# Turning normalized chunks in squares on VectorE instead of with TensorE, split weight-row transfers, and a new order of the last projections, in a two-layer attention and SwiGLU kernel

## The chip, the cores and the metric

The kernel runs on one core of a Trainium2 chip. A core has five engines that work side by side and meet through semaphores: TensorE (PE, with a separate row PEld for weight loads), VectorE (DVE), ScalarE (ACT), GpSimd (POOL) and SyncE (SP). Each has its own queue and takes its instructions in order. Transfers are issued from an engine's queue (here SP's, some from ACT's) and carried by 16 DMA engines. The metric is the device time of one execution in microseconds, as a median over several runs; less is better.

## The reference

Two layers, each of them attention and then a feed-forward part, both with a residual. There are S = 2048 tokens of D = 448 values, H = 16 heads of 28 values that share one key and one value head, and F = 1792 hidden values.

```python
def layernorm(x):                 # no scale, no shift
    return (x - mean(x)) / sqrt(var(x) + 1e-5)

def attention(x):                 # x: 1 x 2048 x 448
    q = (x @ wq) as 16 heads of 28;  k = x @ wk;  v = x @ wv      # one k, one v
    p = softmax(q @ k.T * 28 ** -0.5)
    return (p @ v, heads joined) @ wo

def feed_forward(x):
    return (silu(x @ w_gate) * (x @ w_up)) @ w_down

for layer in range(2):            # the same weights in both layers
    x = x + attention(layernorm(x))
    x = x + feed_forward(layernorm(x))
```

## The kernel before

All products keep fp32 accuracy by splitting an operand a into a high part (rounded to the type fp32r) and a low part a - high, so that a product is three matmuls: high by high, low by high, high by low. The 448 rows of a transposed activation are held as four tiles k = 0 to 3: three of 128 rows, and one whose lower 64 partitions hold the high part and whose upper 64 the low part of the last 64 rows. The last 64 rows of a weight matrix therefore have to stand on both halves of the partitions; `rows3` (lines 128 to 131) loads the first 384 rows in one transfer (line 130) and the last 64 in a second one whose source is read twice through a leading dimension of stride 0 (line 131):

```python
eng.dma_start(dst[:, 3], src[384:448, :][None].to_broadcast([2, 64, n]))
```

The tokens are cut into NC = 4 chunks of 512. `xres` holds the residual with tokens on partitions. `norm_steps` (line 210) gives the steps of a chunk's layernorm: four of statistics on DVE, one scale on POOL, four that apply it on DVE (line 229), each followed by a POOL copy (line 230) that lays the last 64 columns out twice. `flip` (line 241) turns a normalized chunk for PE: per tile k four PE transposes into one PSUM bank (line 246), a copy that makes the high part (line 252, by ACT, or by DVE if a place is given), and a DVE subtraction for the low part (line 253); the last tile has its own copies and subtraction (lines 256 to 262).

*Start.* x arrives in four transfers of tiles and three of chunks (line 887, SP). `load_wqkv` (line 167) loads wq, wk and wv in two halves, one through ACT's queue and one through SP's, with `rows3`; the casts to the high part are ACT's (line 189), the low parts POOL's or DVE's (line 191). Chunk 0 is normalized and turned, then `project` (line 461) runs 16 projections (c, m): of chunk c the m-th 128 columns, in which 112 belong to four heads of queries and 16 to keys (m = 2, 3) or values (m = 0, 1). The order in a chunk is TURN = (3, 2, 0, 1), keys first. Between the projections stand, by a list of numbers (`at`, lines 317 to 326): loads and splits of keys, stacking of queries (`stack`, `parts`), and `rows` (line 386), which puts a bound of the row maxima into the spare rows of the stacked queries by a transfer (line 391); for the first three stacks all three such transfers come at projection 13. `maxima` (line 393) computes the bounds of a chunk; those of chunk c are made while projection 4c + 6 runs. A value piece is turned by DVE (line 505) and put in place by POOL (line 508).

*Attention* (`scores`, line 528) has 16 units (c, g), a chunk by a group of four heads, each of 16 steps over key tiles. A step is 12 matmuls for the scores (line 565), two ACT exponentials of 512 and 1536 columns (lines 571 and 572) and, two steps later, four matmuls by the values (line 602). After a unit the sums are inverted and spread through three transfers (`post`: rs line 618, rd 628, o 629), and POOL scales and splits the result. After a chunk's fourth unit an output projection (`outproj`, line 544, matmuls at 549) runs between two steps, at kt = 10 of units 4, 8 and 12 (`between_steps`, line 575). Inside it, in units 8 and 12, PE also turns chunk 0 for feed-forward (tiles 0 and 1, then 2 and 3), with copies and subtractions on DVE. The norms of chunks 0, 1 and 2 run beside steps of units 5, 13 and 14.

*Feed-forward* takes the 14 slices of F in seven groups of two. A unit (gi, c, n) is one slice for one chunk: 42 matmuls in pairs side by side on the two halves of the partitions (line 292), ACT's silu (line 825), DVE's product, and later the products by w_down. `scores` ends with the units (0,0,0) and (0,0,1) around the output projection of the last chunk; `rest` (line 856) then turns chunk 1 whole (line 863), and chunks 2 and 3 inside the units (0,1,1) and (0,2,1), in the middle between their two halves of matmuls (`mid`). POOL adds two of four residual tiles per chunk and group (line 743).

The order on every engine is that in which the program text issues the instructions.

## Time and profile before

| | us |
|---|---|
| median of three runs | 2038.59 (2035.05 to 2038.96) |
| the profiled execution | 2040.6 |
| its span, from the first to the last instruction | 2038.9 |
| PE busy | 2015.1 (99%) |
| ACT busy | 1310.6 (64%) |
| POOL busy | 537.7 (26%) |
| DVE busy | 457.7 (22%) |
| mean granted clock of TensorE | 0.996 |

A row of the timeline or of the chain gives the start in us, the duration in us, the engine, the line of the kernel, the operation, the output and inputs by the names of the program, and how many instructions lie in it; in brackets stands the idle time of the engine before it and what ended it. "SPq" and "ACTq" are transfers issued from these queues: their time is that of the issue. A row of a table of groups gives the busy time, the mean of one in ns, and the idle time before. A row of a table of stretches gives the stretch, its length, the busy time of PE, PEld, DVE, ACT and POOL, the granted clock, the busy share of the 16 DMA engines and GB/s. In the chain of waits each piece is what the end of the program waited for at that time. An engine that is busy 99% need not be at its peak, since the ends of matmuls are modelled and matmuls overlap.

### The profile page before, as it was taken

To read this page: it belongs to the slowest core of one execution; us is meant where nothing else is said; L and a number is where in the kernel's file an instruction comes from. 1 tells how busy PE (TensorE), PEld (TensorE's weight loads), DVE (VectorE), ACT (ScalarE), POOL (GpSimd) and SP (SyncE) were. 2 spreads that over 40 slices of the span, in tenths; PEclk is the share of its full clock that TensorE was granted. 3 is DMA by queue.
4 is the path that set the end of the run, shared out by engine and by line. 5 is a ranking of instruction groups with operands and counts; after the bars stand their busy time and mean duration, and the time that the engine had idled before them with its cause. 6 is when DMAs were issued, how large, how long until landed. Compare 5 with 4: busy or idle time off the path is not lost.

```text
span 2038.9 us, 43612 instructions
## 1 busy us (share of the span) xinstructions
PE 2015.1 (99%) x18613; PEld 1271.5 (62%) x18613; DVE 457.7 (22%) x890; ACT 1310.6 (64%) x2152; POOL 537.7 (26%) x601
## 2 busy tenths in 40 slices
PE   8999999999999999999999999999999999999998
PEld 6533434334348999999884334343343689988886
DVE  6200101001114323222461001010011242232322
ACT  3699798997973333333348997979979533333332
POOL 4313121021302333333441221111222123333320
PEclk9999999999999999999999999999999999999999
DMA  5201000011100111100031110000110000111101
GB/s 152 60 22 28 21 13 22 12 37 26 32 12 19 31 31 31 30 17 26 22 93 35 30 30 12 22 12 22 28 45 14 28 16 17 31 31 31 31 1 74
DMA packets 76512, 63.44 MB, mean 31 GB/s; under 512 B 22904, under 2 KB 63224, under 8 KB 76312
## 3 DMA queue, kind: packets, MB, share of 16 engines
q1 hardware_dynamic: 74820, 59.39, 10.4%
q8 instruction: 147, 2.41, 0.5%
q10 hardware_dynamic: 1492, 1.20, 0.2%
q14 instruction: 53, 0.43, 0.1%
HBM read 47.72 MB, written 12.32 MB: 29 GB/s over the span
## 4 chain that ended last, share of the span: by engine, by line
PE 50%; ACT 46%; issue 1%; DMA 1%; DVE 1%; SPq 0%; ACTq 0%; POOL 0%; DVEq 0%; POOLq 0%
PE bank L292 39%; ACT pt L572 31%; ACT pt L571 15%; PE bank L272 5%; PE three L549 2%; PE bank L549 2%; PE bank L246 1%; PE bank L602 0%; PE three L565 0%; DMA wr<-in_A_wk_dram 0%; PE bank L398 0%; DMA qstack<-rows 0%; DMA xres<-in_A_x_dram 0%; DVE xl L253 0%; DVE xn L229 0%
## 5 line engine op out<-in xcount | busy, mean ns | idle before, releaser
L572 ACT ACTIVATE pt<-three 128x1536 f32<-128x1536 f32 x512 | 741.1, 1447 | 0.0
L602 PE MATMUL bank<-pt,vsb 128*32 128x512 f32 x4096 | 546.0, 605 | 0.6 <-ACT pt L572 0.6
L565 PEld LDWEIGHTS three<-qstack,keys 32*128 32x128 f32 x4608 | 252.7, 183 | 450.6 <-ACT pt L571 393.6
L565 PE MATMUL three<-qstack,keys 32*128 32x512 f32 x4608 | 497.8, 425 | 4.1 <-DVE vt L505 2.3
L565 PE MATMUL bank<-qstack,keys 32*128 32x512 f32 x1536 | 492.6, 426 | 0.5 <-ACT pt L571 0.5
L292 PE MATMUL bank<-xh,wgh 64*128 64x512 f32 x1728 | 445.4, 390 | 0.4
L292 PE MATMUL bank<-xh,wgl 64*128 64x512 f32 x1404 | 366.8, 390 | 0.0
L571 ACT ACTIVATE pt<-bank 128x512 f32<-128x512 f32 x512 | 306.0, 598 | 71.6 <-PE bank L565 70.5
L292 PE MATMUL bank<-xl,wgh 64*128 64x512 f32 x1296 | 333.4, 390 | 0.0
L292 PE MATMUL bank<-wdh,h 64*128 64x448 f32 x1792 | 330.8, 364 | 1.5 <-ACT h L827 0.8
L292 PEld LDWEIGHTS bank<-xh,wgh 64*128 64x128 f32 x1728 | 260.9, 184 | 19.5 <-DVE xl L253 1.5
L743 POOL TENSOR_TENSOR xres<-stage,xres 128x448 f32<-128x448 f32 x108 | 127.7, 1204 | 497.8 <-ACT stage L742 497.8
L636 POOL TENSOR_TENSOR o<-o 128x512 f32<-128x512 f32 x32 | 41.1, 1284 | 820.4 <-DMA o<-rd 820.4
L292 PEld LDWEIGHTS bank<-wdh,h 64*128 64x128 f32 x1792 | 241.2, 184 | 15.8 <-issue 2.7
L565 PEld LDWEIGHTS bank<-qstack,keys 32*128 32x128 f32 x1536 | 243.9, 183 | 1.3 <-ACT pt L571 1.1
L299 ACT COPY seen<-bank 128x1 f32<-128x1 f32 x664 | 81.6, 163 | 247.8 <-PE bank L292 245.1
L292 PEld LDWEIGHTS bank<-xh,wgl 64*128 64x128 f32 x1404 | 215.1, 184 | 14.2
L292 PE MATMUL bank<-wdl,h 64*128 64x448 f32 x896 | 216.7, 366 | 0.0
L825 ACT ACTIVATE sg<-bank 128x512 f32<-128x512 f32 x112 | 67.3, 601 | 219.5 <-PE bank L292 214.4
L292 PEld LDWEIGHTS bank<-xl,wgh 64*128 64x128 f32 x1296 | 194.8, 184 | 10.5
L602 PEld LDWEIGHTS bank<-pt,vsb 128*32 128x32 f32 x4096 | 80.8, 108 | 189.9 <-issue 174.2
L826 DVE TENSOR_TENSOR sg<-bank,sg 128x512 f32<-128x512 f32 x112 | 77.5, 692 | 499.4 <-ACT sg L825 490.5
(115 smaller groups left out, 1732.1 us busy)
## 6 DMA issues: line engine op xcount, KB each, us to landing
o<-rd SPq DMA_DIRECT2D x32, 256.0 KB
qd<-stage SPq DMA_DIRECT2D x32, 224.0 KB
qraw<-qd SPq DMA_DIRECT2D x128, 56.0 KB
wdr<-in_B_w_down_dram SPq DMA_DIRECT2D x28, 224.0 KB
wr<-in_B_w_gate_dram SPq DMA_DIRECT2D x28, 192.0 KB
wr<-in_B_w_up_dram SPq DMA_DIRECT2D x28, 192.0 KB
out_dram<-xres SPq DMA_DIRECT2D x15, 224.0 KB
xres<-in_A_x_dram SPq DMA_DIRECT2D x3, 896.0 KB
```

The costliest lines, as they stand in the source:

```text
L272: nc.tensor.matmul(po, a, b, start=(i == 0), stop=(i == len(seq) - 1))
L292: nc.tensor.matmul(po, a, b, start=start, stop=stop, skip_group_check=True)
L299: nc.scalar.copy(seen[:, i : i + 1], po[:, 0:1])
L549: nc.tensor.matmul(po[:, 0:D], a[:, g, ts_], b[:, g, :], start=(g + z == 0), stop=(g == NG - 1 and z == 2))
L565: nc.tensor.matmul(three[:, j, :] if j < 3 else one, k[js, kp, ks], q[js, part, :], start=(z == 0), stop=(z == 2), tile_position=(32 * j, 0),)
L571: nc.scalar.activation(pt1, one, AF.Exp, scale=SCALE)
L572: nc.scalar.activation(pt, three, AF.Exp, scale=SCALE)
L602: nc.tensor.matmul(accs[i][32 * j : 32 * j + 32, :], vsb[:, kt, :], pts[n][j], start=(kt == 0), stop=(kt == NT - 1), skip_group_check=True,)
L636: nc.gpsimd.tensor_tensor(rb, oraw, rb, ALU.mult)
L743: nc.gpsimd.tensor_tensor(r, s, r, ALU.add)
L825: nc.scalar.activation(sg, pg[0], AF.Silu)
L826: nc.vector.tensor_tensor(sg, pg[1], sg, ALU.mult)
```

## The change

Chunks 0, 1 and 2 are turned for feed-forward without PE. Their norms run beside the attention steps of units 5 to 6, 9 to 10 and 13 to 14 (from kt = 6 on, one step of the norm beside each attention step). After the four apply steps come four turning steps, one per tile of 128 tokens: DVE transposes the 128 x 448 tile in squares of 32 x 32, and four transfers on SP's queue write the squares to their places in a DRAM tensor of 448 x 512, in pieces of 32 values. `rows3` loads the turned chunk back. Chunk 0 is loaded and split by POOL beside steps of unit 7; chunk 1 is loaded in unit 15 and split in `rest` by ACT (copies) and DVE (subtractions); chunk 2 is loaded in `rest` and split whole by POOL after the unit (0,1,0). Chunk 3 is turned by PE in unit (0,2,1) as before. The POOL copy of the last 64 columns goes for the three chunks.

`rows3` loads the last 64 rows by two transfers to 64 partitions each, everywhere it is used.

The last chunk's projections come in the order LAST = (1, 0, 2, 3), values first; the three transfers of `rows` are issued at projections 9, 11 and 13.

```diff
--- before.py
+++ after.py
@@ -30,6 +30,7 @@
 LEAD = 4
 LIMIT = 2.0**40
 TURN = (3, 2, 0, 1)
+LAST = (1, 0, 2, 3)
 IDLE = 36
 
 
@@ -126,9 +127,9 @@
         nc.sync.dma_start(dst.bitcast(F32), src.bitcast(F32))
 
     def rows3(dst, src, eng=nc.sync):
-        n = src.shape[1]
         eng.dma_start(dst[:, 0:3], src[0:384, :].rearrange("(k p) n -> p k n", p=P))
-        eng.dma_start(dst[:, 3], src[384:448, :][None].to_broadcast([2, 64, n]))
+        for half in (slice(0, 64), slice(64, 128)):
+            eng.dma_start(dst[half, 3], src[384:448, :])
 
     def split(hi, lo, raw):
         nc.gpsimd.tensor_scalar(hi, raw, 1.0, 0.0, ALU.mult, ALU.add)
@@ -207,7 +208,7 @@
             again,
         )
 
-    def norm_steps(c, pool=pers):
+    def norm_steps(c, pool=pers, twice=True):
 
         got = {}
         cs = slice(4 * c, 4 * c + 4)
@@ -227,7 +228,8 @@
                 got["x"] = pool.tile([P, 4, 512], F32, name="xn")
             o, i, r = got["x"][:, t, 0:D], xres[:, 4 * c + t, :], got["r"][:, t : t + 1]
             nc.vector.tensor_scalar(o, i, mv[:, 4 * c + t, 0:1], r, ALU.subtract, ALU.mult)
-            nc.gpsimd.tensor_copy(got["x"][:, t, D:512], o[:, 384:D])
+            if twice:
+                nc.gpsimd.tensor_copy(got["x"][:, t, D:512], o[:, 384:D])
 
         fs = [lambda t=t: stat(t) for t in range(4)] + [scale]
         return fs + [lambda t=t: apply(t) for t in range(4)], got
@@ -261,6 +263,30 @@
             high = xd[64:128, :]
         nc.vector.tensor_tensor(xh[64:128, k, :], pt[64:128, :], high, ALU.subtract)
 
+    def turn_tile(got, tb, raw, t):
+
+        nc.vector.transpose(tb[:, t, :], got["x"][:, t, 0:D])
+        to = raw.rearrange("(b d) (t g w) -> t g d b w", d=32, g=4, w=32)
+        for g in range(4):
+            nc.sync.dma_start(to[t, g], tb[32 * g : 32 * g + 32, t, :].rearrange("d (b w) -> d b w", w=32))
+
+    def halved(tiles, r, ks, copy, sub):
+
+        xh, xl, xd = tiles
+        for k in ks:
+            if k < 3:
+                copy(xh[:, k, :], r[:, k, :])
+                sub(xl[:, k, :], r[:, k, :], xh[:, k, :], ALU.subtract)
+                continue
+            if xd is None:
+                copy(xh[:, 3, :], r[:, 3, :])
+                high = xh[64:128, 3, :]
+            else:
+                copy(xd[64:128, :], r[64:128, 3, :])
+                copy(xh[0:64, 3, :], r[0:64, 3, :])
+                high = xd[64:128, :]
+            sub(xh[64:128, 3, :], r[64:128, 3, :], high, ALU.subtract)
+
     def product_T(po, a_h, a_l, tiles):
 
         xh, xl = tiles[:2]
@@ -307,7 +333,7 @@
             self.layer = layer
             self.X, self.norms, self.qd = {}, {}, {}
             self.done = 0
-            self.order = [(c, m) for c in range(NC) for m in TURN]
+            self.order = [(c, m) for c in range(NC) for m in (TURN if c < NC - 1 else LAST)]
             self.seen = 0
             self.steps, self.places = [], []
             self.lent, self.plan = None, {}
@@ -320,7 +346,7 @@
                 self.at(4 + 3 * i, lambda i=i: self.stack(i))
                 self.at(6 + 3 * i, lambda i=i: self.parts(i))
                 if not full:
-                    self.at(13, lambda i=i: self.rows(i))
+                    self.at((9, 11, 13)[i], lambda i=i: self.rows(i))
             if not full:
                 self.at(2, self.first_keys)
                 self.at(3, self.diagonal)
@@ -464,7 +490,7 @@
             for f in self.plan.get((self.seen, 0), ()):
                 f()
             late = self.layer == 0 and self.seen == 3
-            turned = [o[0] for o in self.order[self.seen : self.seen + 2] if o[1] == 3]
+            turned = [self.order[n][0] for n in (self.seen, self.seen + 1) if n % 4 == 0 and n < len(self.order)]
             for o in turned if not late else ():
                 self.turned(o)
             self.q(c, m)
@@ -584,12 +610,9 @@
                     if not todo or kt != 10:
                         return
                     c = todo.pop()
-                    ks = list({8: (0, 1), 12: (2, 3)}.get(i, ()))
                     adds = []
                     for t in (1, 2, 3):
                         adds.append(outproj(c, t, free[:, t - 1, :]))
-                        if ks:
-                            flip(got, X0, [ks.pop(0)], one)
                     for f in adds:
                         f()
                     outproj(c, 0, one)()
@@ -641,10 +664,40 @@
                     return rest
 
                 X0 = xtile(xpool)
-                fs, got = norm_steps(0)
-                fs1, got1 = norm_steps(1)
-                ff.norms[1] = got1
-                ff.second = norm_steps(2)
+
+                def turns(c, got):
+
+                    at_ = {}
+
+                    def one(t):
+                        if t == 0:
+                            at_["tb"] = wp.tile([P, 4, D], F32, name="tb")
+                        turn_tile(got, at_["tb"], ff.raw[c], t)
+
+                    return [lambda t=t: one(t) for t in range(4)]
+
+                def back():
+
+                    at_ = {}
+
+                    def load():
+                        at_["r"] = pers.tile([P, 4, 512], F32, name="xn")
+                        rows3(at_["r"], ff.raw[0])
+
+                    def part(k):
+                        halved(X0, at_["r"], [k], nc.gpsimd.tensor_copy, nc.gpsimd.tensor_tensor)
+
+                    return [load] + [lambda k=k: part(k) for k in range(4)]
+                aside = {}
+                for c in range(NC - 1):
+                    fs, got = norm_steps(c, twice=False)
+                    ff.raw[c] = dram.tile([D, 512], F32, name=f"xt{self.layer}_{c}")
+                    fs += turns(c, got)
+                    for n, f in enumerate(fs):
+                        aside[16 * (4 * c + 5) + 6 + n] = f
+                for n, f in enumerate(back()):
+                    aside[16 * 7 + 2 + 3 * n] = f
+                aside[16 * 15 + 2] = lambda: ff.fetch(1)
                 last = NT * len(GR)
                 for n in range(last):
                     i, kt = divmod(n, NT)
@@ -671,9 +724,8 @@
                         between_steps(n)
                     if n in due:
                         due.pop(n)()
-                    if i in (5, 13, 14) and kt > 5:
-                        for f in {5: fs, 13: fs1, 14: ff.second[0][:5]}[i][kt - 6 : kt - 5]:
-                            f()
+                    if n in aside:
+                        aside[n]()
                 for n in (last - 2, last - 1):
                     pv(n)
                 self.lent = None
@@ -698,6 +750,7 @@
             self.layer, self.X, self.W, self.norms = layer, {}, {}, {}
             self.pend, self.soon, self.dn, self.flip, self.mid, self.left = [], [], {}, 0, {}, []
             self.nxt = Attention(1) if layer == 0 else None
+            self.raw, self.got = {}, {}
 
         def down(self, fs, fc, d, hh, hl):
 
@@ -776,6 +829,16 @@
             if c < 2:
                 self.mid[len(groups) - 1, c + 2, 0] = [lambda ks=ks: flip(got, a.X[c], ks) for ks in ((0, 1), (2, 3))]
                 self.soon.append([2, lambda: [a.project() for _ in range(2 - c)]])
+
+        def fetch(self, c):
+
+            self.got[c] = pers.tile([P, 4, 512], F32, name="xn")
+            rows3(self.got[c], self.raw[c])
+
+        def parts(self, c, copy, sub):
+
+            self.X[c] = xtile(self.xbp, self.xd[c])
+            halved(self.X[c], self.got.pop(c), range(4), copy, sub)
 
         def turned(self, c, ks=range(4)):
             if c not in self.X:
@@ -860,14 +923,14 @@
             self.xd = [xd.tile([P, 512], F32R, name=f"xd{c}") for c in range(NC)]
             dma(self.xd[0][64:128, :], self.X[0][0][0:64, 3, :])
             self.X[0] = (*self.X[0][:2], self.xd[0])
-            self.turned(1)
-            fs2, self.norms[2] = self.second
+            self.parts(1, nc.scalar.copy, nc.vector.tensor_tensor)
             fs3, self.norms[3] = norm_steps(3)
-            for f in fs2[5:] + fs3[:5]:
+            for f in fs3[:5]:
                 f()
+            self.fetch(2)
+            self.soon.append([0, lambda: self.parts(2, nc.gpsimd.tensor_copy, nc.gpsimd.tensor_tensor)])
             self.soon.append([1, lambda: [f() for f in fs3[5:]]])
-            for c in (2, 3):
-                self.mid[0, c - 1, 1] = [lambda c=c, ks=ks: self.turned(c, ks) for ks in ((0, 1), (2, 3))]
+            self.mid[0, 2, 1] = [lambda ks=ks: self.turned(3, ks) for ks in ((0, 1), (2, 3))]
             for gi, fs in enumerate(groups):
                 if self.layer == 1 and fine is not None and gi in (2, 3):
                     self.verdict(gi == 3)
```

## The prediction

> **What bounds the kernel now.** I read the page's shares first, then the chain of waits, then stretches of the trace around the three kinds of place that the change touches: the start, the two starts of attention, the two passages into feed-forward.
>
> ```profile
> span 2038.9 us, 43612 instructions
> ...
> DMA packets 76512, 63.44 MB, mean 31 GB/s; under 512 B 22904, under 2 KB 63224, under 8 KB 76312
> ...
> q1 hardware_dynamic: 74820, 59.39, 10.4%
> ...
> PE 50%; ACT 46%; issue 1%; DMA 1%; DVE 1%; SPq 0%; ACTq 0%; POOL 0%; DVEq 0%; POOLq 0%
> ```
>
> Half of the chain is PE (projections, feed-forward), the other half is ACT's exponentials in attention; DMA, DVE and POOL hardly appear. So work moved to DVE, POOL or DMA is paid only where it makes PE or ACT wait, and time can be won only where PE or ACT waits now. These stretches show where (PE, weight load, DVE, ACT and POOL busy, then clock, DMA share and GB/s):
>
> ```profile
> 8.00:10.00 2.00, 0.36 (x2) 0.17 (x2) 1.02 (x3) 0.00 (x0) 1.39 (x3) 1.00 0.14 46
> 16.00:22.00 6.00, 5.79 (x13) 4.29 (x14) 5.68 (x11) 3.05 (x7) 2.90 (x9) 0.50 0.56 179
> 74.00:78.00 4.00, 4.00 (x21) 2.00 (x16) 1.28 (x2) 2.44 (x3) 0.58 (x1) 0.50 0.13 34
> 625.00:627.00 2.00, 2.00 (x22) 1.71 (x20) 1.90 (x7) 0.42 (x4) 0.00 (x0) 1.00 0.15 46
> ```
>
> In the first, only the transfers of last weight rows (line 131) are on their way, and 0.14 of the DMA engines' time is used, about 2 of 16; at 625 us, with the same form under way, 0.15. In the second and third PE runs at half clock.
>
> **A. The start.** The chain and the rows of the start:
>
> ```profile
> 5.76 9.54 DMA wr<-in_A_wk_dram
> ...
> 16.21 13.27 PE bank L272 x44
> ```
> ```profile
> 8.02 5.72 SPq L887 DMA_DIRECT2D xres<-in_A_x_dram  x3
> ...
> 13.43 0.94 ACT L189 CAST wh<-wr 128x896 fp32r<-128x896 f32 x1 [5.61 <-DMA wr<-in_A_wq_dram]
> ...
> 14.45 2.50 POOL L191 TENSOR_TENSOR wl<-wr,wh 128x896 fp32r<-128x896 f32 x2 [3.39 <-ACT wh L189]
> 15.38 0.30 ACT L189 CAST wh<-wr 128x128 fp32r<-128x128 f32 x1 [1.01 <-DMA wr<-in_A_wk_dram]
> 15.58 1.55 ACT L252 CAST xh<-bank 128x512 fp32r<-128x512 f32 x3
> ```
> ```profile
> 9.55 2.91 PE L246 MATMUL bank<-ident,xn 128*128 128x128 f32 x16 [2.08 <-DVE xn L229]
> 16.21 0.79 PE L272 MATMUL bank<-xh,wh 128*128 128x512 f32 x1 [3.75 <-ACT xh L252]
> ...
> 29.08 0.39 PE L272 MATMUL bank<-xh,wl 128*128 128x512 f32 x1
> ```
>
> PE has turned chunk 0 by 12.46 and then idles 3.75 us: ACT's copies of xh stand in its queue behind the casts of the weights, and these wait for the two row transfers, landing near 13.3 and 15.3. The change puts two transfers of 64 partitions in the place of each such broadcast. If both spread over all engines, they land soon after the large parts. The large part of wq landed by about 8.0 (the first of the three xres loads, behind it, was issued at 8.02), and the extra issues on ACT's queue, about 0.55 us each, move its table load from 6.33 to about 9. Then the casts run from about 10.5 (0.94 and 0.30), the xh copies start near 11.8 instead of 15.58, wl is there near 14.0 (10.5 + 0.94 + 2.50) and the third matmul, which reads wl, starts near 14.05; it starts at 17.53 now (16.21 + two at half clock). That is 3.5 us. The half clock comes after the idle stretch; with PE's wait cut to short pieces it need not come, and then the 44 matmuls of chunk 0 go at some 0.23 us (those of the end of the row) and end near 23.6 instead of 29.4: 5.8 us. Bounds: 0 (the rows land as late, or the x loads, issued earlier, take the engines) and -6.2; I take -5, nearer the second, since 0.14 busy with both row transfers open leaves them nothing to share. The Trainium skill, "DMA: Bandwidth & Descriptors", Rules for kernel authors, says that a leading broadcast of c copies keeps a DMA to c engines; the shares 0.14 and 0.15 agree with c = 2. In the same table it advises against two transfers to halves of the partitions, since they serialize; by that sentence alone the step would be worth nothing.
>
> Every later weight load has seven issues where it had five, but SP is mostly idle there and the loads lie tens of us ahead: 0.
>
> **B and C. The two starts of attention.** Layer 0, then layer 1:
>
> ```profile
> 66.16 1.94 SPq L391 DMA_DIRECT2D qstack<-rows  x3
> ...
> 70.02 0.59 ACT L498 COPY stage<-bank 128x512 f32<-128x512 f32 x1
> ...
> 71.56 0.50 PE L565 MATMUL three<-qstack,keys 32*128 32x512 f32 x3 [2.06 <-DVE vt L505]
> ```
> ```profile
> 72.57 0.60 ACT L571 ACTIVATE pt<-bank 128x512 f32<-128x512 f32 x1 [1.96 <-PE bank L565]
> ...
> 81.24 0.60 ACT L571 ACTIVATE pt<-bank 128x512 f32<-128x512 f32 x1 [1.01 <-PE bank L565]
> ...
> 83.13 0.60 ACT L571 ACTIVATE pt<-bank 128x512 f32<-128x512 f32 x1
> ```
> ```profile
> 1074.35 2.48 SPq L391 DMA_DIRECT2D qstack<-rows  x3
> ...
> 1080.04 0.51 PE L565 MATMUL three<-qstack,keys 32*128 32x512 f32 x3 [1.76 <-DMA qstack<-rows]
> ...
> 1081.06 0.60 ACT L571 ACTIVATE pt<-bank 128x512 f32<-128x512 f32 x1 [0.76 <-PE bank L565]
> ```
>
> In both, step 0 waits for the first of three row transfers, all issued after projection 13, some 5.5 us before (1074.35 to 1080.04), and for the last V piece on DVE. The change issues them after projections 9, 11 and 13 and puts V ahead of the keys among the last four projections. Then step 0 follows the last projection, and ACT's first exponential follows its last copy: in layer 0 near 70.6 (70.02 + 0.59) for 72.57, 2.0 us. The half clock between 73 and 80 delays steps 1 to 4: the fifth exponential starts at 83.13, while at the later pace of 1.9 us (81.24 to 83.13) it would start at 70.6 + 4 x 1.9 = 78.2. Without the half clock B is thus worth 4.9. Bounds -2.0 and -5.0; I take -4.5, since layer 1 with a gap of 1.76 keeps its clock and here no gap is left. Layer 1: the last copy of ACT has still to wait for its buffer, so the exponential comes at about 1079.4 to 1079.9 instead of 1081.06: bounds -1.0 and -2.0, taken -1.5. The keys of chunk 3 come last now; they are needed at step 12, 12 x 1.9 = 23 us on, and take about 13 (store and load at some 5.6 each, by the row transfer of layer 1, and a POOL split of 1.9, rows under E): 0. The Trainium skill, "TensorE: Matmul & The Clock Gate", Part 1, says that a whole idle window of 3.4 us halves the clock and a busy one restores it. The trace agrees that it is lost after 3.75 us of idling and back some 6.7 us later; a gap of 2.06 costs it in layer 0 and 1.76 does not in layer 1.
>
> **D. Flips of chunk 0 inside the output projections.** The steps without and with flips:
>
> ```profile
> 228.50 0.60 ACT L571 ACTIVATE pt<-bank 128x512 f32<-128x512 f32 x1 [10.35 <-PE bank L565]
> ...
> 361.23 0.60 ACT L571 ACTIVATE pt<-bank 128x512 f32<-128x512 f32 x1 [11.04 <-PE bank L565]
> ```
>
> Here ACT waits for PE, 0.69 us longer with two flips. Four such places go: -2.8 (bounds -2.4 and -3.2).
>
> **E. The passages into feed-forward.** Chunks 1 and 2 come back from DRAM; chunk 3 is still turned by PE.
>
> ```profile
> 618.88 1.91 PE L246 MATMUL bank<-ident,xn 128*128 128x128 f32 x16
> 620.88 1.09 PE L292 MATMUL bank<-xh,wgh 64*128 64x512 f32 x2
> ```
> ```profile
> 627.84 0.60 ACT L825 ACTIVATE sg<-bank 128x512 f32<-128x512 f32 x1 [1.96 <-PE bank L292]
> ...
> 637.58 0.60 ACT L825 ACTIVATE sg<-bank 128x512 f32<-128x512 f32 x1 [1.29 <-PE bank L292]
> ...
> 645.32 0.60 ACT L825 ACTIVATE sg<-bank 128x512 f32<-128x512 f32 x1 [1.96 <-PE bank L292]
> ```
> ```profile
> 630.33 2.33 POOL L743 TENSOR_TENSOR xres<-stage,xres 128x448 f32<-128x448 f32 x2 [1.31 <-ACT stage L742]
> ```
> ```profile
> L134 POOL TENSOR_SCALAR qstack<-qraw 128x512 fp32r<-128x512 f32 x32 | 20.0, 624 | 0.2
> L135 POOL TENSOR_TENSOR qstack<-qraw,qstack 128x512 fp32r<-128x512 f32 x32 | 41.2, 1288 | 2.7
> ```
>
> The 16 transposes before unit (0,1,0) go, but ACT's first copy must wait for the last output projection, whose weights lie in the memory that chunk 1 takes; PE then waits about 1 us instead of turning for 2: -1.0. The 16 transposes inside unit (0,1,1) go too: from silu to silu (line 825) it takes 9.74 us, the next unit without flips 7.74, so -2.0. Against this, POOL splits chunk 2 whole, behind its two adds for chunk 0 (end about 631.6 in the shifted time): three times 0.62 + 1.29, two more copies and a subtraction, 8.3, with gaps some 8.6, so until 640.2. Unit (0,2,0) would begin near 635.6 (1.0 after the silu at 637.58, shifted by 3.0) and needs the third tile's low part seven pairs of matmuls on, at 0.23 each, so at 637.2, where it waits 0.4 (637.6); two pairs later, at 638.1, it needs the last tile and waits 2.1: +2.5. Sum per layer -0.5, bounds -2 (POOL faster than its rows in attention) and +3.5 (the gap of 2.1 halves the clock for some 6.7 us, about 3.4 more, and some tenths of gaps on POOL). Twice: -1, from -4 to +7.
>
> **F. What is added to attention.** Per layer DVE gets 12 transposes (0.72 us by the row of 128x512) and 12 fewer passes at other places; POOL four splits of 1.9 us; SP 48 writes of 448 pieces of 128 bytes. DVE is busy 457.7 us and POOL 537.7 of 2038.9, and a step has 1.9 us set by ACT, so the work itself is hidden. For the writes: 0.104 of 16 engines' 2038.9 us over 74820 packets is 45 ns each; a chunk's 7168 pieces over 16 engines are then 20 us of queue, in a burst of 8 us. Behind it stand qstack loads, which are issued a unit (30 us) ahead, and the chain of sums of an output (rs, rd, o), which has as long before its output projection. Price 0; if each small write took four times as long, the cover would be gone (below).
>
> **Sum.** -5 - 4.5 - 1.5 - 2.8 - 1 + 0 = -14.8 us on the profiled execution of 2040.6 us, which lies 2.0 above the median of 2038.59; I take the sum off the median: 2023.8, told as 2024. A change of 0.2%, 4 us, is about what a measurement of this kernel can tell from none.
>
> **Rivals.**
> 1. *The start gains nothing*, because ACT waits elsewhere or the x loads now compete with the weights: 2024 + 5 = 2029. For it: the row transfer of wk is small and could be late because its queue was, not its engines. The Trainium skill's advice against halves, told above, would end here too.
> 2. *POOL's split of chunk 2 becomes the bound of the passage* and takes the clock with it: +3.5 per layer in the place of -0.5, 2032. For it: POOL is one engine with 8.6 us of work against some 6.5 of cover (631.6 to 638.1).
> 3. *Slower: the small writes hold the queues.* If a 128-byte write costs four times 45 ns, a chunk's burst takes 80 us, and with 30 us for the unit that it falls in and 30 for the next, which the lead of the queries covers, 20 are left in which ACT waits: for six bursts 120, so 2144. It decides from some three times the 45 ns, where a burst outgrows 60 us; 2.3 us beyond that in each eat the whole gain. Against it: 22904 of the packets are under 512 bytes already and the mean is still 45 ns. The Trainium skill, "DMA: Bandwidth & Descriptors", Specifications, has writes under 512 bytes as read-modify-write, which speaks for it; no row here tells their price apart.
> 4. *PE's flips were no bound*: the places of D are filled by other waits: 2024 + 2.8, 2027. Against it: the two rows under D differ by just the flips.
>
> **How the numbers follow.** Chances: the sum as taken, with its terms inside their bounds, 0.50; rival 1, 0.13; rival 2, 0.13; rival 4, 0.07 (all faster); 1 and 2 together, about 2037, no change, 0.06; rival 3 or a milder form of it, 0.11. That gives faster 0.83, same 0.06, slower 0.11. The likeliest case alone spans 2017 to 2030 (A, B and E at their ends, not all at once). Up to 2036 it takes in rivals 1, 2 and 4: range 2016.5 to 2036.
>
> **What would show it.** A: PE's first projection near 12.5 and its 44 near 23.6, no half clock from 16 to 22. B, C: no row transfer before step 0, exponentials near 60 to 65 in shifted time and 1.9 us apart from the first on. D: ACT's idle of 10.35 at all three places of a layer. E: unit (0,1,1) in 7.5 us, then PE waiting for POOL in (0,2,0). F: steps in the units where turns run stay at 1.9 us, and the transfers of rd and qraw land as before; steps longer than that in those units would make the prediction wrong by rival 3.

## The result, and the profile after

The changed kernel takes 2024.96 us (median of five runs, 2024.49 to 2026.19) against 2038.59 for the kernel before. The ratio is 0.9935, with a 95% interval of 0.992 to 0.9949. The forecast was 2024, faster. The profiled execution took 2026.0 us and its span is 2024.3.

These lines of the page of the changed kernel answer to those of before: the span, the packets of all queues, the largest queue (q1, 71.20 of 75.24 MB), and the shares of the chain.

```profile
span 2024.3 us, 43691 instructions
...
DMA packets 126336, 75.24 MB, mean 37 GB/s; under 512 B 69656, under 2 KB 109976, under 8 KB 126136
...
q1 hardware_dynamic: 124584, 71.20, 13.1%
...
PE 48%; ACT 47%; issue 1%; DMA 1%; POOL 1%; DVE 1%; ACTq 0%; POOLq 0%; SPq 0%; DVEq 0%
```

There are 46752 more packets under 512 bytes, and the chain still consists of PE and ACT; POOL has come in with 1%. Where the time went is read by setting marks of the two traces side by side. Each row is the start of the same piece of work; the column before the last is what the stretch up to it gained or lost, and the last one what was forecast for it.

| mark | before | after | shift | this stretch | forecast |
|---|---|---|---|---|---|
| second run of PE flips at the start | 29.31 | 23.88 | -5.43 | A: -5.4 | -5 |
| fifth exponential, layer 0 | 83.13 | 72.63 | -10.50 | B: -5.1 | -4.5 |
| unit (0,0,0) of feed-forward, layer 0 | 595.88 | 583.61 | -12.27 | D and F: -1.8 | -1.4 |
| feed-forward after the passage, layer 0 | 652.51 | 642.43 | -10.08 | E: +2.2 | -0.5 |
| first exponential, layer 1 | 1081.06 | 1069.54 | -11.52 | C: -1.4 | -1.5 |
| unit (0,0,0) of feed-forward, layer 1 | 1601.31 | 1587.85 | -13.46 | D and F: -1.9 | -1.4 |
| feed-forward after the passage, layer 1 | 1657.94 | 1644.02 | -13.92 | E: -0.5 | -0.5 |
| end of the span | 2038.9 | 2024.3 | -14.6 | the rest of feed-forward and the last transfers: -0.7 | 0 |

The start, from PE's timeline and from ACT's:

```profile
12.31 0.50 PE L298 MATMUL bank<-xh,wh 128*128 128x512 f32 x1
13.04 0.51 PE L298 MATMUL bank<-xl,wh 128*128 128x512 f32 x1 [0.23 <-DVE xl L255]
14.23 0.50 PE L298 MATMUL bank<-xh,wl 128*128 128x512 f32 x1 [0.69 <-POOL wl L192]
```
```profile
9.25 1.28 ACT L964 ACT_TABLE_LOAD   x1 [9.25 <-DMA wr<-in_A_wk_dram]
10.54 0.20 ACT L964 ACTIVATE warm<-halfn 128x1 f32<-128x1 f32 x1
10.65 1.12 ACT L190 CAST wh<-wr 128x896 fp32r<-128x896 f32 x2
11.68 1.55 ACT L254 CAST xh<-bank 128x512 fp32r<-128x512 f32 x3
```

The casts start at 10.65 instead of 13.43, and PE's gap of 3.75 us has become two of 0.23 and 0.69. The stretches show the clock; the columns are as in the table of before:

```profile
16.00:22.00 6.00, 6.00 (x28) 4.99 (x27) 4.44 (x14) 2.57 (x5) 2.54 (x6) 1.00 0.65 218
...
74.00:78.00 4.00, 4.00 (x48) 1.32 (x40) 0.00 (x0) 4.00 (x5) 1.52 (x2) 1.00 0.01 2
```

PE runs at full clock in both, where it had 0.50 before. The starts of attention (ACT, layer 0 and layer 1):

```profile
65.07 0.61 ACT L597 ACTIVATE pt<-bank 128x512 f32<-128x512 f32 x1
...
72.63 0.60 ACT L597 ACTIVATE pt<-bank 128x512 f32<-128x512 f32 x1
...
1069.05 0.59 ACT L524 COPY stage<-bank 128x512 f32<-128x512 f32 x1 [0.22 <-DMA qd<-stage]
1069.54 0.60 ACT L597 ACTIVATE pt<-bank 128x512 f32<-128x512 f32 x1
```

No exponential of these waits for PE any more; the first one follows ACT's own last copy. At the output projections ACT waits as long in unit 8, where chunk 0 was turned, as in unit 4, and even a little less (unit 12 as unit 8: 10.08, for 11.02 before):

```profile
217.90 0.60 ACT L597 ACTIVATE pt<-bank 128x512 f32<-128x512 f32 x1 [10.34 <-PE bank L591]
...
349.81 0.60 ACT L597 ACTIVATE pt<-bank 128x512 f32<-128x512 f32 x1 [10.08 <-PE bank L591]
```

The passage into feed-forward lost time in layer 0. PE in unit (0,2,0) waits three times for POOL's split of chunk 2:

```profile
625.71 0.50 PE L318 MATMUL bank<-xl,wgh 64*128 64x512 f32 x2 [1.07 <-POOL xl L279]
627.06 0.71 PE L318 MATMUL bank<-xh,wgh 64*128 64x512 f32 x1 [0.61 <-POOL xh L286]
628.39 0.79 PE L318 MATMUL bank<-xh,wgh 64*128 64x512 f32 x1 [0.63 <-POOL xh L288]
```
```profile
628.00:632.00 4.00, 3.61 (x18) 3.41 (x20) 1.78 (x4) 0.53 (x4) 1.85 (x5) 0.50 0.01 4
1628.00:1632.00 4.00, 1.99 (x13) 0.82 (x9) 0.66 (x1) 0.00 (x0) 3.79 (x4) 1.00 0.00 0
```

The second row of the stretches is layer 1. The same three gaps stand there (1.07, 0.61 and 0.85), and the clock stays at 1.00 in and after them; in layer 0 it falls to 0.50, and unit (0,2,0) takes 13.4 us from silu to silu (621.83 to 635.25) instead of 10.9 (1625.96 to 1636.83).

### The profile page after: what moved, and what is told of

The parts are those of the page before. It is cut to its first block, busy times and chain, and to the rows that moved or that the text cites. A ratio compares the mean times of both kernels' runs of the same rounds, so it can differ in the third digit from the quotient of the medians.

```text
span 2024.3 us, 43691 instructions
## 1 busy us (share of the span) xinstructions
PE 2001.9 (99%) x18517; PEld 1263.2 (62%) x18517; DVE 453.8 (22%) x890; ACT 1305.1 (64%) x2142; POOL 561.4 (28%) x611
## 2 busy tenths in 40 slices
DMA packets 126336, 75.24 MB, mean 37 GB/s; under 512 B 69656, under 2 KB 109976, under 8 KB 126136
## 3 DMA queue, kind: packets, MB, share of 16 engines
q1 hardware_dynamic: 124584, 71.20, 13.1%
## 4 chain that ended last, share of the span: by engine, by line
PE 48%; ACT 47%; issue 1%; DMA 1%; POOL 1%; DVE 1%; ACTq 0%; POOLq 0%; SPq 0%; DVEq 0%
PE bank L318 38%; ACT pt L598 32%; ACT pt L597 15%; PE bank L298 5%; PE three L575 2%; PE bank L575 2%; PE bank L248 1%; POOL xl L279 0%; PE bank L625 0%; DMA qd<-stage 0%; PE three L591 0%; PE bank L424 0%; DMA xn<-xt 0%; DMA xres<-in_A_x_dram 0%; DMA wr<-in_A_wk_dram 0%
```

## The experiments

The theory is the forecast's sum of separate places. Its rivals are that the halves of a transfer gain nothing, that one of the two edits at the start of attention does all, that the PE turns taken out of feed-forward were worth more than POOL's split, and that the small writes hold the queues. All times are medians; the kernel before took 2039.4 to 2040.6 in these groups of runs. The changed kernel was timed in another group, in which the kernel before took 2038.59. So "more than the changed kernel" sets two groups side by side, and a difference of 1 to 2 us told in this way decides nothing without the traces.

### The row transfers alone

```diff
-        eng.dma_start(dst[:, 3], src[384:448, :][None].to_broadcast([2, 64, n]))
+        for half in (slice(0, 64), slice(64, 128)):
+            eng.dma_start(dst[half, 3], src[384:448, :])
```

> The kernel before with only the row transfers split in two halves of 64 partitions. My reading: the broadcast keeps the transfer to 2 of 16 DMA engines, and the two halves use all of them, so the casts of the first weights start near 10.6 us instead of 13.4, PE's 44 projections of chunk 0 end near 24.0 instead of 29.4, no half clock from 16 to 22, and nothing else moves: 5.4 us less, 2033. Rival (halves serialize and gain nothing): the casts start where they did, 2038.6. Second rival (the gain of the start comes from something else in the change): also 2038.6, with the rows landing earlier.

Measured: 2033.86 us against 2039.59, ratio 0.9972 (0.9962 to 0.9982), so 5.7 less. In the stretches of this run the start is that of the changed kernel:

```profile
8.00:10.00 2.00, 0.64 (x5) 0.21 (x3) 1.02 (x3) 0.78 (x1) 1.39 (x3) 1.00 0.26 30
16.00:22.00 6.00, 6.00 (x28) 4.99 (x27) 4.44 (x13) 2.58 (x5) 2.53 (x6) 1.00 0.66 223
1076.00:1080.00 4.00, 4.00 (x16) 2.12 (x16) 0.00 (x0) 3.61 (x4) 2.56 (x5) 0.50 0.12 38
```

The two halves carry the whole of term A. They do so in eight of the nine traced executions of kernels that have them, where the first cast starts at 10.5 to 10.9; the ninth is told below, with the three buffers. The third line is a surprise: this profiled execution (2038.62) lost the clock at the start of attention in layer 1, with a gap of 1.91 us, where the kernel before with 1.76 kept it; the other eight executions took 2032.4 to 2034.8.

The Trainium skill, "DMA: Bandwidth & Descriptors", Rules for kernel authors, advises against two transfers to halves of the partitions. Here the measurement decides otherwise: the choice was between two halves and one broadcast of two copies, which the skill's same table keeps on two engines, and the halves won 5.7 us.

### Early row transfers, values first, and both

```diff
-                    self.at(13, lambda i=i: self.rows(i))
+                    self.at((9, 11, 13)[i], lambda i=i: self.rows(i))
```

> The kernel before with only the three row transfers of the stacked queries issued at projections 9, 11 and 13; the last chunk still projects keys first. My reading: two waits end together at step 0, the row transfer and the last value piece on DVE (71.43 in layer 0), so taking one away leaves the other: step 0 in layer 0 at 71.4 to 71.6 as before, half clock as before; in layer 1 step 0 earlier, but step 1 still behind the value piece at 1081.1, so at most 0.7 us. Sum 0 to -1, 2038. Rival (the row transfer alone was the wait): 2038.6 - 6.5 = 2032.

Measured: 2034.84 us, ratio 0.9977 (0.9967 to 0.9986), 4.8 less. My reading was wrong for layer 0: this edit alone has most of the gain. PE's timeline of this run, layer 0:

```profile
70.00 0.50 PE L565 MATMUL three<-qstack,keys 32*128 32x512 f32 x3
...
72.06 0.50 PE L565 MATMUL three<-qstack,keys 32*128 32x512 f32 x3 [1.09 <-DVE vt L505]
```

Step 0 follows the last projection at once: it never waited for the value piece, though the row of before named DVE. The piece's bank belongs to step 1, which waits 1.09 us for it. A gap of 1.09 instead of 2.06 kept the clock, and the fifth exponential starts at 78.96 instead of 83.13. For layer 1 the reading was right that step 1 stays behind the value piece, and the wait there is longer (PE's timeline, then a stretch):

```profile
1074.19 0.50 PE L565 MATMUL three<-qstack,keys 32*128 32x512 f32 x3
...
1077.20 0.50 PE L565 MATMUL three<-qstack,keys 32*128 32x512 f32 x3 [2.04 <-DVE vt L505]
```
```profile
1078.00:1080.00 2.00, 2.00 (x12) 1.16 (x4) 0.00 (x0) 1.48 (x3) 1.83 (x3) 0.50 0.00 1
```

This execution, the slowest of ten (2037.6, the others from 2033.5), lost the clock after 2.04 us behind the value piece. So the new order has a task of its own: it takes away the wait of step 1, of 1.09 us in layer 0 and 2.04 in layer 1.

```diff
+LAST = (1, 0, 2, 3)
-            self.order = [(c, m) for c in range(NC) for m in TURN]
+            self.order = [(c, m) for c in range(NC) for m in (TURN if c < NC - 1 else LAST)]
```

> The kernel before with only the order of the last chunk's projections changed (values first); the row transfers are all issued at projection 13. My reading: step 0 still waits for the row transfer, 5.5 us after projection 13, so exponentials start where they did (72.6, 1081.1), half clock in layer 0 as before: 0 to -0.5, 2038.4. Rival (the value piece on DVE was the wait, as the row of step 0 in layer 0 says): -5 in layer 0, -1.4 in layer 1, 2032.

Measured: 2037.0 us, ratio 0.9983 (0.9974 to 0.9993), 2.6 less. The ten executions lie from 2033.85 to 2039.44, four of them above 2037.5. The profiled one (2039.14) shows the wait for the row transfer, shorter by 0.7 (the transfers are issued at 65.08 for 66.16), and the half clock after it:

```profile
70.60 0.50 PE L566 MATMUL three<-qstack,keys 32*128 32x512 f32 x3 [1.32 <-DMA qstack<-rows]
```

In layer 1 of the same execution the wait is 1.20 us and the clock is kept. So the gap that remains seems small enough to cost the clock in some executions only. That is an inference from the spread: the others have no trace.

Both diffs together:

> The kernel before with both: early row transfers and values first. My reading: the two waits go together, step 0 follows the last projection, no half clock after it in layer 0 (5.1 us), and 1.4 us in layer 1: 6.5 us less, 2032. If the half clock comes without a gap too, 2.0 + 1.4 = 3.4 less, 2035. If either of the two edits alone gives this, its own run shows it.

Measured: 2033.51 us, ratio 0.9972 (0.9961 to 0.9982), 6.1 less, with exponentials 1.9 us apart from the first one on in both layers. The two edits do not add up to the sum of what each does alone (4.8 and 2.6): each by itself shortens the gap of layer 0 to one that kept the clock (1.09) or seems to keep it in some executions (1.32), and that is won once.

### The changed kernel without its row transfers

```diff
-        for half in (slice(0, 64), slice(64, 128)):
-            eng.dma_start(dst[half, 3], src[384:448, :])
+        eng.dma_start(dst[:, 3], src[384:448, :][None].to_broadcast([2, 64, n]))
```

> The changed kernel with the row transfers as broadcasts again. My reading: the start goes back to the idle of 3.7 us and the half clock, 5.4 us more, 2030.4, and nothing else moves except that the clock may be kept or lost at other places (2.5 either way). Rival (the parts hide one another): less than 3 more.

Measured: 2031.88 us, ratio 0.9958 (0.9942 to 0.9973), 6.9 more than the changed kernel. The half clock of the start is back, and in the profiled execution it also comes in the passage of both layers, with the same three gaps. A is separate from the rest; the surplus of 1.5 is not explained. In the two traces the start makes 5.8 of it all (the first exponential after the output projection of unit 4 comes at 223.72 for 217.90), and the passages, by where the clock is lost, take 1.0 in layer 0 and add 1.5 in layer 1; only one execution of each kernel has a trace.

### Chunk 2: by PE again, and split by two engines

```diff
-            self.fetch(2)
-            self.soon.append([0, lambda: self.parts(2, nc.gpsimd.tensor_copy, nc.gpsimd.tensor_tensor)])
-            self.mid[0, 2, 1] = [lambda ks=ks: self.turned(3, ks) for ks in ((0, 1), (2, 3))]
+            for c in (2, 3):
+                self.mid[0, c - 1, 1] = [lambda c=c, ks=ks: self.turned(c, ks) for ks in ((0, 1), (2, 3))]
...
+            for f in fs2[5:] + fs3[:5]:
```

> The changed kernel with chunk 2 turned by PE inside unit (0,1,1), as in the kernel before; chunks 0 and 1 stay as changed. My reading: 16 transposes come back (2.0 to 2.4 us a layer), the waits for POOL go (2.3 a layer, and 2.5 of half clock in layer 0): together 3 less, about 2022; this piece of the change would then cost time. Rival (the transposes taken away were worth more than POOL's waits): 4 more, 2029.

Measured: 2022.36 us, ratio 0.9915 (0.9901 to 0.9928), 2.6 less than the changed kernel. Taking chunk 2 off PE was a loss, as it was done. The traces agree: from the silu of unit (0,1,0) to that of (0,2,0) it takes 17.48 us here in layer 0 and 17.49 in layer 1, and 20.71 and 18.17 in the changed kernel, so 0.7 more where the clock stays and 3.2 where it falls. If the parts add up, this also prices the turning of chunks 0 and 1: 17.0 less than the kernel before, less 5.7 and 6.1, leaves 5.2 for the four places in the output projections and the two of chunk 1.

```diff
-            self.soon.append([0, lambda: self.parts(2, nc.gpsimd.tensor_copy, nc.gpsimd.tensor_tensor)])
+            self.soon.append([0, lambda: self.parts(2, nc.gpsimd.tensor_copy, nc.vector.tensor_tensor)])
```

> The changed kernel with chunk 2 split by two engines: POOL makes the copies, DVE the subtractions. My reading: in both layers PE waits at unit (0,2,0) for POOL's split (1.07 + 0.61 + 0.63 us), and in layer 0 these three gaps also cost the clock for some 6 us (2.5 us). With five copies of 0.62 on POOL from 619.3 and subtractions of 0.69 on DVE the last tile is there near 622.8, before PE asks for it at 624.6: no wait, no half clock: 2.3 + 2.5 and 2.3, about 7 less than the changed kernel, 2018. If the clock is lost there only in some executions, 5 to 7 less. Rival (the wait is for something other than POOL's subtractions, the loads say, or DVE is as late): no gain, 2025.

Measured: 2017.8 us, ratio 0.989 (0.9875 to 0.9906), 7.2 less than the changed kernel. This beats both kernels. In PE's timeline of this run, from 616 to 640, no row has a wait; DVE's shows the four subtractions:

```profile
619.99 3.10 DVE L279 TENSOR_TENSOR xl<-xn,xh 128x512 fp32r<-128x512 f32 x3 [2.21 <-POOL xh L278]
623.12 0.98 DVE L288 TENSOR_TENSOR xh<-xn,xd 64x512 fp32r<-64x512 f32 x1
624.14 0.69 DVE L889 TENSOR_TENSOR sg<-bank,sg 128x512 f32<-128x512 f32 x1
```

The last tile is there at 624.1 instead of 628.34, and PE reads it at 624.88. In POOL's subtractions lay the 2.3 us of waits in layer 0 and the 2.5 in layer 1, and in layer 0 the 2.5 us of half clock: layer 1 has no wait at this place either, and the clock stays at both.

```diff
+            if c == 1:
+                self.X[2] = xtile(self.xbp, self.xd[2])
-            self.X[c] = xtile(self.xbp, self.xd[c])
+            if c not in self.X:
+                self.X[c] = xtile(self.xbp, self.xd[c])
```

> The kernel with chunk 2 split by POOL and DVE, and with chunk 1's tiles for feed-forward in the second of three buffers instead of the first. My reading: the first copy of chunk 1 waits for the last output projection only because its tile lies where the weights of that projection lie (0.71 + 0.23 us of PE idle a layer); if the second buffer is free earlier, the copies run beside the projection and PE goes on at once: 1.9 less, 2016. Rival (the second buffer lies under something that is needed as long): 2017.8, no change.

Measured: 2017.28 us, ratio 0.989 (0.9875 to 0.9905): no change against the kernel it is built on. PE still waits 0.71 us ahead of unit (0,1,0), for a copy that still waits for the last output projection. The rival fits, but what lies under the second buffer stays open.

The profiled execution (2019.69, the others 2017.1 to 2017.5) shows something else, at the start. ACT's cast of wk, then PE's first projection:

```profile
14.03 0.30 ACT L190 CAST wh<-wr 128x128 fp32r<-128x128 f32 x1 [1.83 <-DMA wr<-in_A_wk_dram]
```
```profile
14.86 0.80 PE L298 MATMUL bank<-xh,wh 128*128 128x512 f32 x1 [2.08 <-ACT xh L254]
```

The two halves of wk were issued at 8.72 here, 0.6 us later than in the changed kernel's trace (8.10), while the loads of x followed at 9.29 for 9.15; from 12 to 14 the DMA engines are busy throughout in both. PE's first projection is 2.6 us later than there (12.31), and the clock, which fell to 0.50 during the transposes, is at 0.50 from 12 to 18. This looks like the forecast's first rival, x loads that compete with the weights, in one of nine traced executions; that the x loads are the reason is not shown.

### What the small writes cost

```diff
-        for g in range(4):
+        for g in (0, 1, 2, 3) * 4:
             nc.sync.dma_start(to[t, g], tb[32 * g : 32 * g + 32, t, :].rearrange("d (b w) -> d b w", w=32))
```

> The changed kernel with every square written four times over to the same place (192 transfers of 448 pieces of 128 bytes a layer for 48, more work than needed). My reading: a write costs some 17 ns of a DMA engine by the difference of the two profiles, so four times a chunk's writes are 30 us of queue and 38 us of issues on SP, and the lead of one to two units (30 us each) still covers them: 0 to 2 more, up to 2027. The rival of small writes that hold the queue: some 20 us more for each burst that outgrows 60 us, 2050 to 2150.

Measured: 2048.94 us, ratio 1.0043 (1.0028 to 1.0059), 24 more than the changed kernel and more than the 2 expected. SP's timeline of this run during the turning of chunk 0, then that of the changed kernel:

```profile
252.89 20.19 SPq L271 DMA_DIRECT2D xt<-tb  x32
273.12 2.48 SPq L641 DMA_DIRECT2D rs<-o  x4
275.70 19.93 SPq L271 DMA_DIRECT2D xt<-tb  x32
295.67 0.48 SPq L651 DMA_DIRECT2D rd<-rs  x1
```
```profile
252.93 4.05 SPq L271 DMA_DIRECT2D xt<-tb  x8
261.44 2.47 SPq L641 DMA_DIRECT2D rs<-o  x4
264.03 4.46 SPq L271 DMA_DIRECT2D xt<-tb  x8
268.60 0.44 SPq L651 DMA_DIRECT2D rd<-rs  x1
```

The row sums of unit 4 (rs, then rd) stand in SP's queue between and behind the squares. With four writes rd is issued 27 us late, and the units after it make up a part of that. In the output projection of unit 8 PE waits 6.39 us for POOL's split of the result, the clock falls to 0.50, and ACT's idle is 9.6 us longer than the 10.08 of the changed kernel:

```profile
359.10 0.60 ACT L597 ACTIVATE pt<-bank 128x512 f32<-128x512 f32 x1 [19.70 <-PE bank L591]
```

The same places of unit 12 and of layer 1 add 1.9, 7.7 and 2.4 us, and the passage of layer 1, which loses its clock here, 2.5. The next runs ask whether SP's issues or the DMA engines are to blame.

```diff
+            for _ in range(3):
+                nc.sync.dma_start(to[t, g][:, 0, :], tb[32 * g : 32 * g + 32, t, 0:32])
```

> The changed kernel with as many transfers as when every square is written four times (192 a layer), but the added 144 write only one block of 32 x 32 each, 32 pieces for 448. It tells SP's issues from the writes themselves. My reading after the run with four full writes (24 more): there SP issued for 43 us on end and the row sums of the unit came out behind it, while the pieces cost some 14 ns of an engine each, 25 us a chunk; so it is SP's queue, and this kernel loses as much, 2045 to 2049. Rival (the small writes hold the DMA engines): most of the 24 us go, 2025 to 2030.

Measured: 2311.29 us, ratio 1.133 (1.1309 to 1.135). This run does not compare as meant: each added transfer writes into a place just written and waits until that has landed, 1.3 us in the mean (362.5 us over 288 waits), with all of SP's queue behind it. SP then issues from 253.1 to 339.8, 87 us. It does show that few pieces (138408 packets in all against 258216 with four full writes) and a queue occupied for longer cost far more than many pieces in a queue occupied for less.

```diff
+    spare = dram.tile([6 * 48, 32, 32], F32, name="spare")
...
+            for z in range(3):
+                nc.sync.dma_start(spare[made[0] + 12 * t + 3 * g + z], tb[32 * g : 32 * g + 32, t, 0:32])
```

> As the kernel with 144 added small writes a layer, but these go to places of their own in a spare tensor, so that none waits for another to land. SP issues 64 transfers a chunk, as with four full writes, and the DMA engines get 16 x 448 + 48 x 32 = 8704 pieces for 28672. If SP's queue is what held the row sums (my reading), SP is busy some 25 to 43 us on end and the loss is like that of four full writes or somewhat less, 10 to 24, so 2035 to 2049. If the small writes hold the DMA engines, nearly all of the loss goes, 2025 to 2028.

Measured: 2032.97 us, ratio 0.9965 (0.9952 to 0.9978), 8.0 more than the changed kernel: below the 10 to 24 that I expected, and above the rival's. In the trace it is 5.7 more, of which the output projections make 3.6 (2.5 in layer 0, 1.0 in layer 1), and the clock in the two passages 1.5. The stretch from 281 to 285, in the middle of the burst, the issue of rd and the wait at unit 8 follow:

```profile
281.00:285.00 4.00, 4.00 (x48) 1.31 (x40) 0.00 (x0) 4.00 (x5) 0.00 (x0) 1.00 0.24 38
```
```profile
290.49 0.37 SPq L658 DMA_DIRECT2D rd<-rs  x1
```
```profile
352.54 0.60 ACT L604 ACTIVATE pt<-bank 128x512 f32<-128x512 f32 x1 [12.61 <-PE bank L598]
```

The DMA engines are busy a quarter of the time in this stretch, and rd is still issued 22 us late, and ACT's idle at the output projection is 2.5 us longer. The transfers behind rd are not slower either. POOL's product of unit 4 waits for them, in the changed kernel and with four full writes:

```profile
275.68 1.29 POOL L659 TENSOR_TENSOR o<-o 128x512 f32<-128x512 f32 x1 [25.15 <-DMA o<-rd]
```
```profile
302.69 1.28 POOL L659 TENSOR_TENSOR o<-o 128x512 f32<-128x512 f32 x1 [52.20 <-DMA o<-rd]
```

From the issue of rd to this product it is 7.1 and 7.0 us, and 6.9 with the spare tensor (290.49 to 297.39). So the burst delays the chain only by holding back the issue of rd in SP's queue, and the loss follows that time: 268.6 (changed kernel), 290.5 (8 more), 295.7 (24 more), 339.8 (286 more).

```diff
-        for g in range(4):
+        for g in (0, 1, 2, 3) * 2:
```

> The changed kernel with every square written twice: 32 transfers a chunk, some 22 us of SP for 12, and 14336 pieces. It asks how much cover the turning has. With four writes the row sums came 27 us late and the output projection waited 9.5 us, so some 17 us are covered; with two the row sums are late by some 10: 0 to 1 more than the changed kernel, 2025 to 2026. If the cover is less than one such burst: 4 to 8 more, 2030.

Measured: 2026.2 us, ratio 0.9935 (0.9918 to 0.9951), 1.2 more than the changed kernel, in another group of runs; the two profiled spans are 2024.4 and 2024.3. rd is issued at 275.4, 7 us late, and no wait at an output projection grows (10.10 for 10.08 in unit 8). The cover is between 7 and 22 us of SP's queue beyond what the changed kernel uses.

## Why the prediction was right, and where not

**The sum.** -14.8 was forecast for the profiled execution and -14.6 came. That it came so near is luck: B and D gave 1.5 more than said and A 0.4, E gave 2.7 less in layer 0, and the end added 0.7 that nothing in the change explains. The mechanisms of A, C and D and of E's waits are those of the forecast; one sentence under B and the price of D failed, and the half clock of E came in one layer only.

**A** (-5; -5.4 in the trace, -5.7 alone) came step by step: casts near 10.5 (10.65), xh copies near 11.8 (11.68), the third matmul near 14.05 (14.23), no half clock. The rival that the start gains nothing is out for the median by its own run; one traced execution in nine had a late transfer of wk, as this rival has it.

**B** (-4.5; -5.1) was right in size, but the forecast's sentence that step 0 also waits for the last value piece on DVE failed. With early row transfers alone step 0 follows at once in both layers; the value piece held step 1, by 1.09 us in layer 0 and 2.04 in layer 1. The row of step 0 named the engine whose event came last, and the other layer's row named the transfer; the run with one edit decided it.

**C** (-1.5; -1.4) came as worked out: ACT's last copy waits for its buffer (0.22), then the exponential.

**D** (-2.8; -3.7 with F) was mis-sized: the two rows set unit 8 with flips beside unit 4 without, but unit 8 without flips is quicker than unit 4 (10.08 for 10.34), so a place was worth 0.94 to 1.08, 4.0 in all, and not 0.69. Rival 4 is out with it.

**E** is where rival 2 came true in one of two layers. POOL's split ended at 628.34; the forecast's 640.2, less the 12.3 that the trace is ahead there, is 627.9. The waits sum to 2.3 and 2.5 for a forecast of 2.5, and where the clock stays the layer comes out at -0.5, as said (layer 1). That the gap halves the clock was kept as a bound and a rival, at 3.4 us; it measured 2.5 from silu to silu, in layer 0 alone. The run with PE turning chunk 2 and the run with DVE subtracting show both halves of the account. The forecast's own terms for chunk 2, -2.0 and +2.5, already made this piece a loss.

**F** (0): set against the 4.0 of D, the stretches with turns lose some 0.1 to 0.2 us a layer. Rival 3 was right to look at SP and the small writes, but its mechanism failed: a write costs 17 ns of an engine by the two profiles ((0.131 x 2024.3 - 0.104 x 2038.9) x 16 over the 49764 packets that q1 has more), less than half the mean of 45 that the forecast took, and 14 by the run with four writes. What decides is the 0.5 to 0.6 us that SP takes for each issue, and the cover is not the 60 us that the rival allowed but some 7 to 22 beyond the present use.

## What to carry to other kernels

A transfer that reads its source twice through a leading dimension of two used 0.14 to 0.15 of the sixteen engines here, about two of them; two plain transfers cost one more issue and ended the wait, which matters where the first work of a program hangs on it. Work moved from the engine on the path to one off it is only free if the new engine is done in time at the one place that reads it: here POOL alone took 9.0 us (619.34 to 628.34), and PE first stood still for it at 624.6, so that chunk 2's turns, worth some 4.6 us over both layers to PE (2022.36 against 2017.8), became a loss of 2.6; a second engine brought the gain back. Before adding many small transfers to a queue, look for the short chain (here sums, spread, product) whose transfers stand in the same queue, and count the issues, not the bytes.

## What the hardware showed unexpectedly

The clock. Where PE waited 3.75 to 4.39 us at the start (the kernel before and three runs), the profiled execution lost it. After shorter gaps it went either way. At the starts of attention 1.09 and 1.20 us kept it and 1.32 lost it; 1.76 in the kernel before kept it; 1.91, 2.04, 2.06 and 2.10 lost it. Behind a wait of 2.08 ahead of the first transposes the kernel before kept it through them; behind 2.10 and 2.25 it fell during them in two runs. The three gaps of 1.07, 0.61 and some 0.6 to 0.85 within 4 us stand in six traced kernels: in layer 0 five of them lost the clock, in layer 1 four. The Trainium skill, "TensorE: Matmul & The Clock Gate", Part 1, speaks of a free-running window of 3.4 us that must be idle. A window that runs freely fits the chance between executions; that it must be idle throughout does not fit gaps of 2 us and less that lost it.

VectorE and GpSimd slowed each other by more than the forecast allowed for. A POOL subtraction of 128 x 512 takes 1.29 us alone and 1.77 while DVE works on a tile of the same size with both inputs in SBUF, the memory that these engines share (DVE's subtraction at 623.84, line 893). Beside a DVE product that reads one input from PSUM, where PE's results lie (at 622.47, line 889), it takes 1.30. POOL's rows in the changed kernel:

```profile
621.95 1.30 POOL L279 TENSOR_TENSOR xl<-xn,xh 128x512 fp32r<-128x512 f32 x1
...
623.89 1.77 POOL L279 TENSOR_TENSOR xl<-xn,xh 128x512 fp32r<-128x512 f32 x1
```

When DVE took the subtractions of chunk 2 beside POOL's copies, they lasted 1.09 us each in the mean, where the same ones for chunk 1, beside ACT's copies, take 0.69 in the changed kernel. The Trainium skill, "GPSIMD Engine Reference", 1. Specifications, says that the two share their SBUF interfaces and contend where a DVE instruction has two SBUF inputs, as these have; the rows agree. Here it is some 0.5 us on top of 1.3 for POOL and 0.4 on top of 0.7 for DVE.
